# Half of each unit's attention moved beside the older unit's gate/value matmuls, with ScalarE's copies left to the scheduler

## The chip, the cores and the metric

One core of one Trainium2 chip runs the whole program. The metric is the device time of one execution in microseconds (us); the median of the runs is what the prediction is about.

## What is computed

A gated linear recurrence over 4 batches, 8 heads and 768 time steps of width 48 feeds a GEGLU block with a gated residual over 3072 tokens of width 384:

```
mag = sqrt(a_re² + a_im²);  a = (a_re + i·a_im) · min(mag, 0.999) / (mag + 1e-6)
S_t = a_t ∘ S_{t-1} + k_t v_tᵀ          (complex state, 48×48 per head)
x_t = q_t · Re(S_t)                      (heads side by side: 384 numbers per token)
out = x + sigmoid(x w_res) · ((gelu(x w_gate) · (x w_val)) w_out)      (d_ff 1536)
```

## The kernel before

The recurrence is done as attention within chunks of 128 tokens, with a carried state between chunks. A **chunk** is 128 tokens of all 8 heads; a **group** g is two chunks; a **unit** u is two groups, that is four chunks or 512 tokens. There are 6 units, 12 groups (3 to a batch) and 24 chunks. The program walks u from -2 to 6 and traces two stages for each value, `phase_x(u)` (called the **X stage** here) and `phase_y(u)` (the **Y stage**).

The X stage of u holds work for four units at once. For u+2 it makes the logarithm of the magnitude (`lm`) and the tangent of the phase (`th`), lines 148 to 171: six table functions of ScalarE for each group (Ln, Exp, Square, Ln, later Arctan), with VectorE's products between. For u+1 it makes the running sums along time by matmul (`csl`, `cst`, lines 174 to 210), their exponentials `E` and `Ei`, the reduced phases `fg`, and at the end the Sin functions `CS` (lines 212 to 217). For each group of u+1 that is not the first of its batch it sends three rows through DRAM on GpSimd's DMA queue (`md`, then `m3`, printed as `m_` with a number, lines 219 to 237) to get the factor `M` by which the carried state is brought to the new group's origin. For u it runs the attention of all four chunks (lines 260 to 338), and for u-1 the output matmuls `op` (lines 382 to 392).

Attention of one chunk is two half-chunks of four heads. Each transposes Q and K on TensorE into one PSUM tile `tp`, which ScalarE and VectorE copy in turn into `qk` (lines 278 and 279); then TensorE makes the scores `at`, VectorE masks them into `atm` (line 286), and TensorE makes `y`. `tp`, `at` and `y` have one PSUM buffer each. ScalarE casts `y` to `x`, TensorE transposes it (`tpx`), and ScalarE or VectorE copies it into `xT` (lines 351 and 353), the input of the dense block. `dk` is the state's new part, `G` and `Gb` the carried state.

The Y stage of u runs the gate/value matmuls of u: 12 steps of three matmuls into `gp` and three into `vp` (lines 355 to 370, 128 by 512 each), a Gelu on ScalarE and a product on VectorE for each, and four steps `rp` for the residual gate. `gp`, `vp`, `rp`, `op`, `csl` and `cst` share four PSUM buffers. The Y stage also makes the products for u+1 on VectorE (`qE`, `kE`, `Q`, `K`, lines 239 to 257) and issues the loads.

ScalarE needs three table sets in turn: logarithm and exponential, Arctan and Sin, Gelu and Tanh; each switch is an ACT_TABLE_LOAD (line 397). The order of work is set as follows. `weave` (line 17) sorts steps by a position in the stage; a scheduler then orders every engine's instructions when the program is built, except ScalarE's, which `tc.manual_schedule` (line 452) keeps in the traced order, its copies included. SP issues the loads of q, k, a_re (`ar`) and a_im (`ai`) and the stores, GpSimd those of v, the weights and `md`. At the start SP's queue holds `ar` and `ai` of groups 0 to 3 and then q and k.

Of the kernel before, what the change touches and what calls it, by code (L numbers as in the profile page):

```python
# [28 lines left out]
def kernel(  # L29
# [118 lines left out]
    def p1_steps(g):  # L148
        def s0():
            T["lm", g] = pA.tile([128, W], FP, tag="lm", name="lm")  # L150
            nc.scalar.activation(out=T["lm", g], in_=flat(T["ar", g]), func=AF.Ln)  # L151

        def s1():
            T["th", g] = pA.tile([128, W], FP, tag="th", name="th")
            nc.scalar.activation(out=T["th", g], in_=T["lm", g], func=AF.Exp, scale=-1.0)  # L155
            nc.vector.tensor_tensor(out=T["th", g], in0=T["th", g], in1=flat(T["ai", g]), op=OP.mult)  # L156

        def s2():
            T["s", g] = pS.tile([128, W], FP, tag="s", name="s")
            nc.scalar.activation(out=T["s", g], in_=T["th", g], func=AF.Square)  # L160

        def s3():
            nc.scalar.activation(out=T["s", g], in_=T["s", g], func=AF.Ln, bias=1.0)
            lm = T["lm", g]
            nc.vector.scalar_tensor_tensor(out=lm, in0=T["s", g], scalar=0.5, in1=lm, op0=OP.mult, op1=OP.add)
            nc.vector.tensor_scalar(out=lm, in0=lm, scalar1=LNMAX, scalar2=None, op0=OP.min)  # L166

        return [s0, s1, s2, s3]

    def p1_arctan(g):  # L170
        nc.scalar.activation(out=T["th", g], in_=T["th", g], func=AF.Arctan)


    def cs_l(g, c):
        if c == 0:
            T["E", g] = pE.tile([128, W], FP, tag="E", name="E")
            T["Ei", g] = pE.tile([128, W], FP, tag="Ei", name="Ei")
        sl = slice(c * DM, (c + 1) * DM)
        cs = psM.tile([128, DM], FP, tag="mm", padded_shape=[128, 512], name="csl")
        nc.tensor.matmul(out=cs, lhsT=lmat[c], rhs=T["lm", g][:, sl], start=True, stop=True)  # L180

        def ex():
            nc.scalar.activation(out=T["E", g][:, sl], in_=cs, func=AF.Exp)
            nc.scalar.activation(out=T["Ei", g][:, sl], in_=cs, func=AF.Exp, scale=-1.0)  # L184
        return ex
# [26 lines left out]
    def p2_sin(g):  # L212
        T["CS", g] = pQ.tile([128, C * H, 2, D], BF, tag="CS", name="CS")

        nc.scalar.activation(out=T["CS", g][:, :, 0], in_=T["fg", g][:, :, 0], func=AF.Sin, scale=2.0 * math.pi,
                             bias=hpi)
        nc.scalar.activation(out=T["CS", g][:, :, 1], in_=T["fg", g][:, :, 1], func=AF.Sin, scale=2.0 * math.pi)

    def decay(g):
# [40 lines left out]
    def attention(g, c):  # L260
        s = g % NS
        first = s == 0 and c == 0
        Q = T["Q", g].rearrange("p x u d -> p x (u d)")
        K = T["K", g].rearrange("p x u d -> p x (u d)")
        V = T["v", g]
        st = {}

        def grp(hg):
            def a():
                tp = psT.tile([128, 1024], BF, tag="tp", name="tp")  # L270
                for j in range(4):
# [16 lines left out]
            return a  # L288

        def dk():  # L290
            if s == NS - 1 and c == C - 1:
# [4 lines left out]
            for h in range(H):  # L296
                nc.tensor.matmul(out=d[0:DD, h * D:(h + 1) * D], lhsT=K[:, c * H + h], rhs=V[:, c, h],
                                 start=(c == 0 and h == 0), stop=(h == H - 1), skip_group_check=True)

        def yy():  # L300
            y = psY.tile([128, DM], FP, tag="y", padded_shape=[128, 512], name="y")
            for h in range(H):
                ys = y[:, h * D:(h + 1) * D]
                hg, j = divmod(h, 4)
                nc.tensor.matmul(out=ys, lhsT=st["atm", hg][:, j], rhs=V[:, c, h], start=True, stop=first)  # L305
                if not first:
# [4 lines left out]
            T["x", g * C + c] = x  # L311

        def state():
            if s == NS - 1 and c == C - 1:
                return
            d = T["dk", g][0:DD].rearrange("p (h d) -> p h d", h=H)
            Gb = stt.tile([128, H, D], BF, tag="Gb", name="Gb")
            if c == 0:
                if s == 0:
# [35 lines left out]
    def gv_step(u, ffi):  # L355
# [12 lines left out]
        nc.scalar.activation(out=h2[:, ffi, :], in_=gp, func=AF.Gelu)  # L368
        nc.vector.scalar_tensor_tensor(out=h2[:, ffi, :], in0=h2[:, ffi, :], scalar=0.5, in1=vp,
                                       op0=OP.mult, op1=OP.mult)  # L370

    def rp_step(u, jj):
# [7 lines left out]
        nc.scalar.activation(out=T["sg", u][:, jj], in_=rp, func=AF.Tanh, scale=0.5)  # L380

# [13 lines left out]
    def table(nm):  # L395
        def f():
            nc.scalar.preload_act_table_set(nm)  # L397
        return f
# [7 lines left out]
    def zip_steps(lists):  # L406
        return [st for tup in zip(*lists) for st in tup]

    def phase_x(u):

# [5 lines left out]
        def ex():  # L416
            pend.pop(0)()
        front = []
        for g in gs(u + 1):
            for c in range(C):  # L420
                front.append(call(csl, g, c))
        p1 = zip_steps([p1_steps(g) for g in gs(u + 2)])
# [4 lines left out]
        trig = [table("trig_and_small")] + [call(p1_arctan, g) for g in gs(u + 2)] + [call(p2_sin, g) for g in gs(u + 1)]  # L427
        att = [st for g in gs(u) for c in range(C) for st in attention(g, c)]
        ops = [call(op_step, u - 1, jj) for jj in range(4)] if 0 <= u - 1 < NU else []
        xts = []  # L430
        if gs(u):
            att2 = []
            for i in range(4):
                att2 += att[4 * i:4 * i + 4] + [call(xt_step, u, i)]
            att = att2
        if p1 or exs:
            table("natural_log_exp_and_others")()
        weave((0.0, 0.12, front), (0.05, 0.55, p1), (0.15, 0.5, exs), (0.5, 0.5, dec), (0.25, 0.7, cst),
              (0.69, 0.69, dec2), (0.7, 0.95, trig), (0.0, 1.0, att), (0.1, 1.1, ops))

    def phase_y(u):
# [6 lines left out]
        pr = [st for g in gs(u + 1) for st in products(g)]  # L448
        lds = [call(load_a, g) for g in gs(u + 4)] + [call(load_q, g) for g in gs(u + 3)]
        weave((0.0, 1.0, gv), (0.0, 0.8, pr), (0.0, 0.6, lds))  # L450

    with tc.manual_schedule(engines={mybir.EngineType.Activation}):
        for g in gs(0) + gs(1):
            load_a(g)
        for g in gs(0):
            load_q(g)
        for u in range(-2, NU + 1):
            phase_x(u)
            if u == -2:
                for g in gs(1):  # L460
                    load_q(g)
                load_w()
            phase_y(u)

# [29 lines left out]
```

## Time and profile before

| what | value |
|---|---|
| time, median of 3 runs | 428.3 us (427.64 to 428.71) |
| time of the profiled execution | 427.52 us |
| its span, first to last instruction | 425.8 us |
| busy: TensorE, VectorE, ScalarE | 72%, 60%, 49% of the span |
| start to the first X stage with attention (u = 0) | 71 us |
| X stage of u = 0, which has no `op` beside it | 44.5 us |
| from the first gate/value matmul of one unit to that of the next | 57.8, 59.3, 58.6, 54.8, 48.4 us |
| last Y stage and last four `op` steps | 18.6 and 12.8 us |

A stage is read from the trace by the first gate/value matmul of its unit and the last residual matmul. Busy time of TensorE counts pipelined matmuls by their full latency, so start-to-start distances tell more there. The granted clock is TensorE's mean clock as a share of 2.4 GHz; the two levels are 1.2 and 2.4 GHz.

### The profile page before, as it was taken

The page shows a single profiled execution, that of the slowest core. Times are in us where ns is not written, and L with a number is a line of the kernel's source. Part 1 is how long each engine was busy: PE and PEld are TensorE (multiplying, and loading weights), DVE is VectorE, ACT ScalarE, POOL GpSimd, SP SyncE. Part 2 cuts the span into 40 slices and gives each one's busy share as a digit, 9 for nine tenths or more (in the row PEclk, how much of TensorE's full clock was granted, in tenths as well). Part 3 has the DMA queues.
Part 4 walks back from the last instruction along what each step waited for, and adds up shares of the span by engine and source line. Part 5 has one row for each costly group of instructions (what it writes and reads, how often), then busy time and mean ns, then how long its engine had stood idle before and what let it go on. Part 6 is the DMA issues. An engine that isn't in the chain of part 4 may idle for free.

```text
span 425.8 us, 5538 instructions
## 1 busy us (share of the span) xinstructions
PE 307.9 (72%) x2080; PEld 176.0 (41%) x2080; DVE 254.7 (60%) x452; ACT 209.7 (49%) x342; POOL 58.5 (14%) x88
## 2 busy tenths in 40 slices
PE   0040361664699895898966997958989879975996
PEld 0020121443445463445544455634456534654353
DVE  1310385578853598744898435997536974672344
ACT  1530618454746657457447366574553555424450
POOL 9330150022100240100311002100004000000000
PEclk9985585575599898799985898976998969995799
DMA  9999999999860791802364500211001100010002
GB/s 140 158 201 174 164 155 182 185 156 166 140 62 2 130 147 42 94 0 39 79 57 95 70 0 1 76 49 26 0 3 21 38 20 0 20 57 0 1 2 74
DMA packets 145146, 32.22 MB, mean 76 GB/s; under 512 B 139360, under 2 KB 144352, under 8 KB 145120
## 3 DMA queue, kind: packets, MB, share of 16 engines
q1 hardware_dynamic: 111616, 25.17, 34.8%
q0 software_dynamic: 33504, 6.70, 18.6%
q8 instruction: 16, 0.26, 0.3%
q14 instruction: 10, 0.08, 0.1%
HBM read 33.69 MB, written 4.76 MB: 90 GB/s over the span
## 4 chain that ended last, share of the span: by engine, by line
PE 54%; DVE 18%; issue 8%; DMA 8%; ACT 8%; POOL 3%; DVEq 0%; POOLq 0%; ACTq 0%
PE gp L362 13%; PE vp L366 12%; PE op L386 8%; DMA wr<-in_moe_w_res_dram 4%; DVE atm L286 3%; PE cst L200 3%; PE at L283 3%; PE rp L378 3%; PE csl L180 2%; DMA v<-in_v_dram 2%; PE tp L273 2%; PE tp L276 2%; PE cst L202 2%; DVE qk L279 2%; POOL v L132 2%
## 5 line engine op out<-in xcount | busy, mean ns | idle before, releaser
L362 PE MATMUL gp<-xT,wg 128*128 128x512 bf16 x216 | 65.2, 415 | 2.7 <-DVE xT L353 2.7
L366 PE MATMUL vp<-xT,wv 128*128 128x512 bf16 x216 | 63.8, 407 | 0.0
L278 ACT COPY qk<-tp 96x512 bf16<-96x512 bf16 x48 | 27.9, 581 | 47.0 <-PE tp L276 46.9
L156 DVE TENSOR_TENSOR th<-th,ai 128x768 f32<-128x768 f32 x12 | 11.5, 958 | 47.2 <-ACT th L155 40.3
L286 DVE TENSOR_TENSOR atm<-at,mask_81 128x512 bf16<-128x512 f32 x48 | 33.0, 687 | 10.3 <-PE at L283 10.2
L283 PE MATMUL at<-qk 96*128 96x128 bf16 x192 | 22.1, 248 | 22.4 <-DVE qk L279 22.2
L362 PEld LDWEIGHTS <-wg 128*128 128x128 bf16 x216 | 22.7, 105 | 31.4 <-issue 11.3
L366 PEld LDWEIGHTS <-wv 128*128 128x128 bf16 x216 | 22.5, 104 | 30.1 <-issue 8.1
L310 ACT CAST x<-y 128x384 bf16<-128x384 f32 x24 | 11.5, 479 | 47.5 <-PE y L307 39.9
L273 PE MATMUL tp<-ident,Q 128*96 128x128 bf16 x192 | 22.3, 249 | 17.1 <-DVE Q L254 9.8
L279 DVE COPY qk<-tp 96x512 bf16<-96x512 bf16 x48 | 20.0, 417 | 23.8 <-ACT qk L278 23.7
L132 POOL DMA_DIRECT2D v<-in_v_dram x28 | 25.1, 905 | 51.9 <-PE y L307 46.6
L200 PE MATMUL cst<-th,lt0b 128*128 128x384 f32 x24 | 13.1, 631 | 22.1 <-ACT Ei L184 21.7
L273 PEld LDWEIGHTS <-Q 128*96 128x96 bf16 x192 | 19.2, 148 | 23.4 <-issue 11.0
L397 ACT ACT_TABLE_LOAD x22 | 28.2, 1283 | 1.1 <-PEq L478 0.7
L283 PEld LDWEIGHTS <-qk 96*128 96x128 bf16 x192 | 13.4, 108 | 34.8 <-DVE qk L279 33.1
L180 PE MATMUL csl<-lm,lt0a 128*128 128x384 f32 x24 | 11.3, 556 | 22.7 <-DVE lm L166 22.7
L151 ACT ACTIVATE lm<-ar 128x768 f32<-128x768 f32 x12 | 10.1, 842 | 31.8 <-DMA ar<-in_a_re_dram 31.8
L305 PE MATMUL y<-v,atm 128*128 128x48 bf16 x192 | 17.8, 196 | 10.6 <-DVE atm L286 10.6
L276 PE MATMUL tp<-ident,K 128*96 128x128 bf16 x192 | 22.5, 251 | 0.2 <-DVE K L254 0.2
L223 POOL DMA_DIRECT2D md<-Ei x8 | 4.0, 506 | 123.2 <-ACT Ei L184 123.2
L305 PEld LDWEIGHTS <-atm 128*128 128x128 bf16 x192 | 12.9, 103 | 19.1 <-DVE atm L286 17.5
(124 smaller groups left out, 641.5 us busy)
## 6 DMA issues: line engine op xcount, KB each, us to landing
q<-in_q_dram SPq DMA_DIRECT2D x28, 192.0 KB, 4.6
k<-in_k_dram SPq DMA_DIRECT2D x28, 192.0 KB, 4.7
ar<-in_a_re_dram SPq DMA_DIRECT2D x24, 192.0 KB, 4.5
ai<-in_a_im_dram SPq DMA_DIRECT2D x24, 192.0 KB, 4.9
out_dram<-ot SPq DMA_DIRECT2D x24, 192.0 KB, 1.9
v<-in_v_dram POOLq DMA_DIRECT2D x28, 96.0 KB, 6.1
wg<-in_moe_w_gate_dram POOLq DMA_DIRECT2D x3, 384.0 KB, 14.7
wv<-in_moe_w_val_dram POOLq DMA_DIRECT2D x3, 384.0 KB, 15.5
```

Of the source, the lines that this page charges most:

```text
L132: nc.gpsimd.dma_start(out=t[:, c], in_=rows(v, g, c))
L273: nc.tensor.transpose(out=tp[0:DD, j * 128:j * 128 + 128], in_=Q[:, x], identity=ident)
L276: nc.tensor.transpose(out=tp[0:DD, 512 + j * 128:640 + j * 128], in_=K[:, x], identity=ident)
L278: nc.scalar.copy(out=qk[0:DD, 0:512], in_=tp[0:DD, 0:512])
L279: nc.vector.tensor_copy(out=qk[0:DD, 512:1024], in_=tp[0:DD, 512:1024])
L283: nc.tensor.matmul(out=at[:, j], lhsT=qk[0:DD, 512 + j * 128:640 + j * 128], rhs=qk[0:DD, j * 128:j * 128 + 128], start=True, stop=True)
L286: nc.vector.tensor_tensor(out=atm, in0=at, in1=mask4, op=OP.mult)
L305: nc.tensor.matmul(out=ys, lhsT=st["atm", hg][:, j], rhs=V[:, c, h], start=True, stop=first)
L362: nc.tensor.matmul(out=gp, lhsT=wg[:, fi, ffi * 128:(ffi + 1) * 128], rhs=xT[:, fi, :], start=(fi == 0), stop=(fi == KD - 1))
L366: nc.tensor.matmul(out=vp, lhsT=wv[:, fi, ffi * 128:(ffi + 1) * 128], rhs=xT[:, fi, :], start=(fi == 0), stop=(fi == KD - 1))
L386: nc.tensor.matmul(out=ps, lhsT=h2[:, ffi, jj * 128:(jj + 1) * 128], rhs=wo[:, ffi, :], start=(ffi == 0), stop=(ffi == KF - 1))
L397: nc.scalar.preload_act_table_set(nm)
```

## The change

Attention is cut by groups. The first group of unit u+1 (two chunks, 256 tokens) is traced in the Y stage of u, from 0.3 to 0.95 of it; the second group of u stays in the X stage of u, from 0 to 0.8. The products for u+1 are pressed into the first 0.4 of the Y stage. All attention steps are given high priority in the scheduler. `tc.manual_schedule` goes: ScalarE's instructions are scheduled like the others', only that a chain of added dependences without semaphores (`tab`) keeps table loads and all table functions in traced order; plain copies (`qk`, `x`, `xT`) are free. The carried state is multiplied by `M` at the entry of the next group (`enter`) and not at the end of the last one. Pools: `x` 8 to 10 buffers, `xT` 1 to 2, `m3` and `M` 2 to 3. SP's first loads now go a group at a time: `ar`, `ai`, q, k of group 0, then of group 1, then the rest. Every table function of ScalarE is traced through the helper `act` (so the changed kernel's rows for them show its line, L120).

```diff
+    def tab(ins):
+        if "tab" in T:
+            tc.add_manual_dep(ins.ins, T["tab"].ins.name, order, reason="table order")
+        T["tab"] = ins
+
+    def act(**kw):
+        tab(nc.scalar.activation(**kw))
...
+        def hi(f):
+            def w():
+                with tc.high_priority():
+                    f()
+            return w
+        return [hi(f) for f in (enter, grp(0), dk, grp(1), yy)]
...
+    def att_steps(u, half):
+        steps = []
+        for g in gs(u)[half:half + 1]:
+            for c in range(C):
+                steps += attention(g, c)
+                steps.append(call(xt_step, u, half * C + c))
+        return steps
...
-        weave((0.0, 0.12, front), (0.05, 0.55, p1), (0.15, 0.5, exs), (0.5, 0.5, dec), (0.25, 0.7, cst),
-              (0.69, 0.69, dec2), (0.7, 0.95, trig), (0.0, 1.0, att), (0.1, 1.1, ops))
+        weave((0.0, 0.12, front), (0.05, 0.55, p1), (0.12, 0.45, exs), (0.46, 0.46, dec), (0.25, 0.65, cst),
+              (0.69, 0.69, dec2), (0.7, 0.95, table_trig), (0.0, 0.8, att_steps(u, 1)), (0.1, 1.0, ops))
...
-        weave((0.0, 1.0, gv), (0.0, 0.8, pr), (0.0, 0.6, lds))
-    with tc.manual_schedule(engines={mybir.EngineType.Activation}):
+        weave((0.0, 1.0, gv), (0.0, 0.4, pr), (0.3, 0.95, att_steps(u + 1, 0)))
+    for g in gs(0):
+        load_a(g)
+        load_q(g)
+    for g in gs(1):
+        load_a(g)
+    for g in gs(1):
+        load_q(g)
...
```

**ScalarE in the X stage of u = 1.** Before, from the last two `E` to the first of the Sin functions; the copies `qk`, `xT` and the cast `x` belong to attention.

```order
L183 ACTIVATE E<-csl 128x384
L184 ACTIVATE Ei<-csl 128x384
L163 ACTIVATE s<-s 128x768 x2
L278 COPY qk<-tp 96x512 x2
L310 CAST x<-y 128x384
L233 ACTIVATE m_1210<-m_1210 96x8
L233 ACTIVATE m_1217<-m_1217 96x8
L397 ACT_TABLE_LOAD
L351 COPY xT<-tpx 128x3x128
L171 ACTIVATE th<-th 128x768
L278 COPY qk<-tp 96x512
L171 ACTIVATE th<-th 128x768
```

The changed kernel in the same place, from the third pair of `E` and `Ei`:

```order
L120 ACTIVATE Ei<-csl 128x384
L120 ACTIVATE s<-th 128x768
L372 COPY xT<-tpx 128x3x128
L120 ACTIVATE s<-th 128x768
L120 ACTIVATE E<-csl 128x384
L295 COPY qk<-tp 96x512
L120 ACTIVATE Ei<-csl 128x384
L120 ACTIVATE s<-s 128x768 x2
L295 COPY qk<-tp 96x512
L120 ACTIVATE m_1258<-m_1258 96x8
L120 ACTIVATE m_1265<-m_1265 96x8
L418 ACT_TABLE_LOAD
```

The stage has four copies `qk` in place of eight, each with table functions between it and the next; between the third `Ei` and the first `m_` row six table functions, two copies `qk` and one `xT` stand.

**TensorE and VectorE in the Y stage of u = 1.** Before, VectorE's row for the Gelu products of this unit comes once, then one `Gb`, then 11 times without anything between. In the changed kernel attention of u = 2 stands between; TensorE first (rows that repeat are left out), then VectorE:

```order
L293 MATMUL tp<-ident,K 96x128
...
L300 LDWEIGHTS qk
L300 MATMUL at<-qk 128x128
...
L387 LDWEIGHTS wv
L387 MATMUL vp<-xT,wv 128x512
...
L338 LDWEIGHTS atm
L338 MATMUL y<-v,atm 128x48
L340 LDWEIGHTS qk
L340 MATMUL y<-Gb,qk 128x48
```

```order
L390 SCALAR_TENSOR_TENSOR h_1413<-h_1413,vp 128x512 x2
L351 TENSOR_TENSOR Gb<-dk,G 96x384
L296 COPY qk<-tp 96x512
L390 SCALAR_TENSOR_TENSOR h_1413<-h_1413,vp 128x512
L316 TENSOR_TENSOR G<-dk,G 96x384
L303 TENSOR_TENSOR atm<-at,mask_81 128x512
L317 TENSOR_TENSOR G<-G,M 96x384
L296 COPY qk<-tp 96x512
L390 SCALAR_TENSOR_TENSOR h_1413<-h_1413,vp 128x512
L303 TENSOR_TENSOR atm<-at,mask_81 128x512
L253 TENSOR_TENSOR qE<-q,E 128x768
```

Gate/value matmuls stand between a step of attention and the step that needs its result, on TensorE; on VectorE copies, masks and products stand between the Gelu products.

**SP's loads at the start.** Before:

```order
L121 DMA ar_151<-in_a_re_dram 128x8x48 x2
L121 DMA ai_154<-in_a_im_dram 128x8x48 x2
L121 DMA ar_157<-in_a_re_dram 128x8x48 x2
L121 DMA ai_160<-in_a_im_dram 128x8x48 x2
L121 DMA ar_163<-in_a_re_dram 128x8x48 x2
L121 DMA ai_166<-in_a_im_dram 128x8x48 x2
L121 DMA ar_169<-in_a_re_dram 128x8x48 x2
L121 DMA ai_172<-in_a_im_dram 128x8x48 x2
L128 DMA q_175<-in_q_dram 128x8x48 x2
```

The changed kernel (`ar_188` is group 3's):

```order
L132 DMA ar_152<-in_a_re_dram 128x8x48 x2
L132 DMA ai_155<-in_a_im_dram 128x8x48 x2
L139 DMA q_158<-in_q_dram 128x8x48 x2
L139 DMA k_161<-in_k_dram 128x8x48 x2
L132 DMA ar_167<-in_a_re_dram 128x8x48 x2
L132 DMA ai_170<-in_a_im_dram 128x8x48 x2
L139 DMA q_173<-in_q_dram 128x8x48 x2
L139 DMA k_176<-in_k_dram 128x8x48 x2
L132 DMA ar_182<-in_a_re_dram 128x8x48 x2
L132 DMA ai_185<-in_a_im_dram 128x8x48 x2
L132 DMA ar_188<-in_a_re_dram 128x8x48 x2
```

The loads of q and k of groups 0 and 1, eight transfers, stand ahead of `ar` of group 2 where they stood behind `ai` of group 3.

## Rows read from the trace of the kernel before

**Rows 1.** Windows by stage: us, busy of PE, PEld, DVE, ACT, POOL (instructions), PEclk, DMA, GB/s
```profile
71.00:115.50 44.50, 26.39 (x216) 19.58 (x217) 34.04 (x61) 25.36 (x42) 6.19 (x9) 0.58 1.15 163
...
133.50:173.30 39.80, 31.40 (x268) 19.89 (x266) 30.97 (x60) 25.55 (x44) 8.55 (x12) 0.87 0.57 86
173.30:191.30 18.00, 18.00 (x79) 7.99 (x79) 9.69 (x14) 8.29 (x15) 0.50 (x1) 0.92 0.47 54
...
251.80:291.20 39.40, 30.58 (x270) 20.43 (x269) 31.26 (x60) 25.35 (x42) 3.72 (x6) 0.84 0.17 41
...
310.00:346.00 36.00, 30.01 (x268) 19.43 (x267) 26.21 (x53) 18.48 (x34) 4.93 (x7) 0.92 0.10 24
...
364.80:394.40 29.60, 21.87 (x242) 15.02 (x241) 16.13 (x31) 10.72 (x18) 0.00 (x0) 0.83 0.08 28
```

**Rows 2.** Waits of the whole span: who waited for whom: us in total, times, longest
```profile
ACT qk L278 <- PE tp L276: 46.9, 28, 3.9
...
ACT x L310 <- PE y L307: 39.9, 20, 3.4
...
PE at L283 <- DVE qk L279: 22.2, 19, 3.3
...
PE y L305 <- DVE atm L286: 10.6, 16, 1.1
```

**Rows 3.** Groups by line: busy us, mean ns of one, idle before
```profile
L286 DVE TENSOR_TENSOR atm<-at,mask_81 128x512 bf16<-128x512 f32 x48 | 33.0, 687 | 10.3 <-PE at L283 10.2
...
L278 ACT COPY qk<-tp 96x512 bf16<-96x512 bf16 x48 | 27.9, 581 | 47.0 <-PE tp L276 46.9
...
L279 DVE COPY qk<-tp 96x512 bf16<-96x512 bf16 x48 | 20.0, 417 | 23.8 <-ACT qk L278 23.7
...
L310 ACT CAST x<-y 128x384 bf16<-128x384 f32 x24 | 11.5, 479 | 47.5 <-PE y L307 39.9
```

**Rows 4.** Timeline, ScalarE and GpSimd, stage X of u = 2: start, us, instruction
```profile
206.91 0.50 ACT L184 ACTIVATE Ei<-csl 128x384 f32<-128x384 f32 x1
...
210.30 0.87 POOL L227 DMA_DIRECT2D m_1858<-md  x1 [2.11 <-DVE qE L242]
```

**Rows 5.** View of the tile m_1858, its last line
```profile
DMA to landing us min/median/max: 4.4/4.4/4.4
```

**Rows 6.** Timeline of TensorE, stages X and Y of u = 2
```profile
203.92 0.39 PE L273 MATMUL tp<-ident,Q 128*96 128x128 bf16 x4
204.14 0.39 PE L276 MATMUL tp<-ident,K 128*96 128x128 bf16 x4
...
207.19 0.20 PE L305 MATMUL y<-v,atm 128*128 128x48 bf16 x1
207.22 0.18 PE L307 MATMUL y<-Gb,qk 96*128 96x48 bf16 x1
...
235.06 1.48 PE L362 MATMUL gp<-xT,wg 128*128 128x512 bf16 x3
...
242.22 0.81 PE L366 MATMUL vp<-xT,wv 128*128 128x512 bf16 x3
242.87 0.81 PE L362 MATMUL gp<-xT,wg 128*128 128x512 bf16 x3
```

**Rows 7.** Windows of 2 us in the stage X of u = 2, columns as in rows 1
```profile
206.00:208.00 2.00, 2.00 (x23) 1.21 (x22) 2.00 (x6) 2.00 (x5) 0.65 (x2) 1.00 0.28 99
...
222.00:224.00 2.00, 0.61 (x7) 0.50 (x6) 1.85 (x4) 1.99 (x3) 0.00 (x0) 0.50 0.30 108
```

**Rows 8.** Timeline of the start, SP's queue and ScalarE
```profile
44.42 4.62 SPq L128 DMA_DIRECT2D q<-in_q_dram  x2
46.65 0.84 ACT L151 ACTIVATE lm<-ar 128x768 f32<-128x768 f32 x1 [11.67 <-DMA ar<-in_a_re_dram]
...
55.15 2.77 SPq L128 DMA_DIRECT2D q<-in_q_dram  x2
...
65.57 0.21 ACT L233 ACTIVATE m_330<-m_330 96x8 f32<-96x8 f32 x1 [10.64 <-DMA m_330<-md]
```

More of the change, by code (lines that the diff above doesn't have):

```diff
@@ L109 @@
     T = {}
+    order = mybir.DependencyInfo(mybir.DependencyClass.NoSync, mybir.DependencyReason.DATA)
+    def tab(ins):
[4 more added lines that the diff above has]
+        tab(nc.scalar.activation(**kw))
     def rows(a, g, c):
@@ L170, in p1_arctan @@
     def p1_arctan(g):
-        nc.scalar.activation(out=T["th", g], in_=T["th", g], func=AF.Arctan)
+        act(out=T["th", g], in_=T["th", g], func=AF.Arctan)
     def cs_l(g, c):
@@ L182, in ex @@
         def ex():
-            nc.scalar.activation(out=T["E", g][:, sl], in_=cs, func=AF.Exp)
-            nc.scalar.activation(out=T["Ei", g][:, sl], in_=cs, func=AF.Exp, scale=-1.0)
+            act(out=T["E", g][:, sl], in_=cs, func=AF.Exp)
+            act(out=T["Ei", g][:, sl], in_=cs, func=AF.Exp, scale=-1.0)
         return ex
@@ L213, in p2_sin @@
         T["CS", g] = pQ.tile([128, C * H, 2, D], BF, tag="CS", name="CS")
-        nc.scalar.activation(out=T["CS", g][:, :, 0], in_=T["fg", g][:, :, 0], func=AF.Sin, scale=2.0 * math.pi,
+        act(out=T["CS", g][:, :, 0], in_=T["fg", g][:, :, 0], func=AF.Sin, scale=2.0 * math.pi,
                              bias=hpi)
-        nc.scalar.activation(out=T["CS", g][:, :, 1], in_=T["fg", g][:, :, 1], func=AF.Sin, scale=2.0 * math.pi)
+        act(out=T["CS", g][:, :, 1], in_=T["fg", g][:, :, 1], func=AF.Sin, scale=2.0 * math.pi)
     def decay(g):
@@ L288, in grp, with enter @@
             return a
+        def enter():
+            if s == 0 or c > 0:
+                return
+            d = T["dk", g - 1][0:DD].rearrange("p (h d) -> p h d", h=H)
+            Mb = T["M", g][0:DD].rearrange("p (h u) -> p h u", u=1).to_broadcast([DD, H, D])
+            G = stt.tile([128, H, D], FP, tag="G", name="G")
+            if s == 1:
+                nc.vector.tensor_tensor(out=G[0:DD], in0=d, in1=Mb, op=OP.mult)
+            else:
+                nc.vector.tensor_tensor(out=G[0:DD], in0=d, in1=T["G"][0:DD], op=OP.add)
+                nc.vector.tensor_tensor(out=G[0:DD], in0=G[0:DD], in1=Mb, op=OP.mult)
+            Gb = stt.tile([128, H, D], BF, tag="Gb", name="Gb")
+            nc.vector.tensor_copy(out=Gb[0:DD], in_=G[0:DD])
+            T["G"] = G
+            T["Gbf"] = Gb
         def dk():
@@ L296, in dk @@
             for h in range(H):
-                nc.tensor.matmul(out=d[0:DD, h * D:(h + 1) * D], lhsT=K[:, c * H + h], rhs=V[:, c, h],
+                nc.tensor.matmul(out=d[0:DD, h * D:(h + 1) * D], lhsT=K(c * H + h), rhs=V(h),
                                  start=(c == 0 and h == 0), stop=(h == H - 1), skip_group_check=True)
@@ L304, in yy @@
                 hg, j = divmod(h, 4)
-                nc.tensor.matmul(out=ys, lhsT=st["atm", hg][:, j], rhs=V[:, c, h], start=True, stop=first)
+                nc.tensor.matmul(out=ys, lhsT=st["atm", hg][:, j], rhs=V(h), start=True, stop=first)
                 if not first:
@@ L311, in yy @@
             T["x", g * C + c] = x
[L313 to L317, printed above, removed]
             if c == 0:
+                d = T["dk", g][0:DD].rearrange("p (h d) -> p h d", h=H)
+                Gb = stt.tile([128, H, D], BF, tag="Gb", name="Gb")
                 if s == 0:
@@ L367, in gv_step @@
                              start=(fi == 0), stop=(fi == KD - 1))
[L368 removed]
+        act(out=h2[:, ffi, :], in_=gp, func=AF.Gelu)
         nc.vector.scalar_tensor_tensor(out=h2[:, ffi, :], in0=h2[:, ffi, :], scalar=0.5, in1=vp,
@@ L379, in rp_step @@
                              start=(fi == 0), stop=(fi == KD - 1))
-        nc.scalar.activation(out=T["sg", u][:, jj], in_=rp, func=AF.Tanh, scale=0.5)
+        act(out=T["sg", u][:, jj], in_=rp, func=AF.Tanh, scale=0.5)
     def op_step(u, jj):
@@ L417, in ex @@
             pend.pop(0)()
[L418 to L421, printed above, removed]
+        front = [call(csl, g, c) for g in gs(u + 1) for c in range(C)]
         p1 = zip_steps([p1_steps(g) for g in gs(u + 2)])
@@ L427, in phase_x @@
         trig = [table("trig_and_small")] + [call(p1_arctan, g) for g in gs(u + 2)] + [call(p2_sin, g) for g in gs(u + 1)]
-        att = [st for g in gs(u) for c in range(C) for st in attention(g, c)]
         ops = [call(op_step, u - 1, jj) for jj in range(4)] if 0 <= u - 1 < NU else []
[L430 to L435, printed above, removed]
         if p1 or exs:
             table("natural_log_exp_and_others")()
-        weave((0.0, 0.12, front), (0.05, 0.55, p1), (0.15, 0.5, exs), (0.5, 0.5, dec), (0.25, 0.7, cst),
-              (0.69, 0.69, dec2), (0.7, 0.95, trig), (0.0, 1.0, att), (0.1, 1.1, ops))
+            table_trig = trig
+        else:
+            table_trig = []
+        weave((0.0, 0.12, front), (0.05, 0.55, p1), (0.12, 0.45, exs), (0.46, 0.46, dec), (0.25, 0.65, cst),
+              (0.69, 0.69, dec2), (0.7, 0.95, table_trig), (0.0, 0.8, att_steps(u, 1)), (0.1, 1.0, ops))
     def phase_y(u):
@@ L448, in phase_y @@
         pr = [st for g in gs(u + 1) for st in products(g)]
-        lds = [call(load_a, g) for g in gs(u + 4)] + [call(load_q, g) for g in gs(u + 3)]
-        weave((0.0, 1.0, gv), (0.0, 0.8, pr), (0.0, 0.6, lds))
-    with tc.manual_schedule(engines={mybir.EngineType.Activation}):
-        for g in gs(0) + gs(1):
-            load_a(g)
[L455 to L463, printed above, removed]
+        weave((0.0, 1.0, gv), (0.0, 0.4, pr), (0.3, 0.95, att_steps(u + 1, 0)))
[6 more added lines that the diff above has]
+        load_q(g)
+    for u in range(-2, NU + 1):
+        phase_x(u)
+        if u == -2:
+            load_w()
+        phase_y(u)
+        for g in gs(u + 4):
+            load_a(g)
+        if u >= -1:
+            for g in gs(u + 3):
+                load_q(g)
 _INS = ['q', 'k', 'v', 'a_re', 'a_im', 'moe_w_gate', 'moe_w_val', 'moe_w_out', 'moe_w_res']
```

50 lines of the change are left out of this document (20 added, 30 removed).

## The prediction

> **What bounds the kernel now.** I read four views in this order. The windows by stage come first [rows 1]: in an X stage no engine is full. Take those of u = 1 and u = 3 (that of u = 2, between them, is alike): in 39.4 to 39.8 us TensorE is busy for some 31, VectorE for some 31, ScalarE for 25.5. In the Y stage of u = 1 TensorE is busy all 18.0 us, VectorE 9.7, ScalarE 8.3. So the Y stage is TensorE's, with room on the two others, and the X stage belongs to something that is not busy time.
>
> The list of waits says to what [rows 2]. ScalarE, which ran in traced order, waited 46.9 us for the transposes `tp` before its copies `qk` and 39.9 us for `y` before its casts `x`. That is 86.8 us over 24 chunks, 3.6 us for each, 14.5 us for the four of an X stage. Busy 25.5 and waits 14.5 make 40.0, which is the stage's length. The X stage is ScalarE's queue: a copy that waits for TensorE holds up every table function behind it, and a table function holds up the copy on which TensorE's next step waits. From the first gate/value matmul of u = 0 to that of u = 3 (115.5 to 291.2 us [rows 1]) there are three periods of one Y and one X stage: 175.7 us, 58.6 each.
>
> **The change, part by part.** The sum is made against the profiled execution, 427.5 us (span 425.8 and 1.7 around it), 0.8 below the median of the runs.
>
> *X stage, u = 1 to 3.* Two of four chunks leave it. ScalarE loses four `qk` of 0.58, two `x` of 0.48 [rows 3] and one `xT` that I count as an `x`: 3.8 us, so 21.7 are left. The waits for the two chunks that stay would be 7.2 us at the old price; by the order of the changed kernel each `qk` now has table functions before the next, and only table functions must keep their order. The bounds are 0 and 7.2; I take half, 3.6, since nothing in the trace says how well the scheduler's idea of a duration fits. A wait shows that the long stage hid: the factor that comes back through DRAM. In u = 2 the `Ei` ended at 207.4; the first `m3` transfer was issued at 210.3, the second 0.87 later, and landed 4.4 after that, at 215.6 [rows 4, 5]: 8.2 us. In the changed order there stand between this `Ei` and the `m_` row four table functions of 0.84 (the `lm` row has their size [rows 8]), `E` and `Ei` of 0.5 [rows 4], two `qk` and one `xT`: 6.0 us. ScalarE then waits 2.2 ahead of the Sin table. Sum: 21.7 + 3.6 + 2.2 = 27.5 us. VectorE loses 4 × (0.69 + 0.42) = 4.4 [rows 3] of its 31 and part of the products, so it stays just under that; TensorE is below both. Bounds: 23.9 (no attention wait) and 31.1 (7.2 of it).
>
> *Y stage, u = 0 to 4.* TensorE's 18.0 stay. As `gp` and `vp` share four buffers, two steps (four tiles, 0.65 each from start to start [rows 6]) can run while ScalarE is still at the Sin functions: 2.6 off, since `xT` of u is now ready earlier than the tables are. Two chunks come in. At full clock four transposes start 0.22 after the four before them, and one `y` matmul 0.03 after another [rows 6]; a chunk has 27 matmuls of 128 columns and 24 of 48: 1.5 + 0.7 = 2.2 us, two chunks 4.4. TensorE runs in order and so waits where a result is late: before, 22.2 us for `qk` and 10.6 for `atm` [rows 2] over 48 half-chunks, 0.7 each; four make 2.7. Sum: 18.0 − 2.6 + 4.4 + 2.7 = 22.5. VectorE's load there is 9.7 + 4.4 and part of the products, and stays below. Lower bound 19.8 (no waits). Upper bound: two chunks at the price that one has when it stands nearly alone, 29.6 / 4 = 7.4 in the X stage of u = 5 [rows 1]: 18.0 − 2.6 + 14.8 = 30.2. I take 22.5 because the order puts gate/value matmuls between each attention step and its user, as nothing did in u = 5.
>
> A rule speaks against this stage. The row first: with attention, `op` and `cst` mixed, TensorE was granted full clock in 206 to 208 us, and half in 222 to 224, where it was busy only 0.61 of 2 us [rows 7]. The Trainium skill (TensorE: Matmul & The Clock Gate, section A second HAM failure mode: psum-queue depth-cycling) says that frequent short idles between groups of 512-column matmuls make the clock swing between its levels. By it the Y stage would lose its full clock; by the row it keeps it as long as TensorE stays busy.
>
> A period is then 27.5 + 22.5 = 50.0 instead of 58.6: three times 8.6, **−25.8 us**.
>
> *Y of u = 3 and X of u = 4.* X was 36.0 with ScalarE busy 18.5 [rows 1]; 14.7 are left. There is no work for later units, so less covers the DRAM trip, and two factors are wanted: I put 7 for that wait and 1.8 for attention, 23.5. With Y 46.0 against 54.8: **−8.8**.
>
> *Y of u = 4 and X of u = 5.* X was 29.6 us for four chunks with little beside them; two cost 14.8, with 1.2 for the handover 16.0. With Y 38.5 against 48.4: **−9.9**. Two of the table loads go here as well, inside this term.
>
> *X of u = 0.* Nothing runs beside it, so all four chunks stay in line. The two halves of its ScalarE order are freer: at most the 14.5 us of waits, at least nothing. VectorE is busy 34.0 of 44.5 [rows 1], which caps the gain at 10. I take **−5**.
>
> *Start.* q and k of groups 0 and 1 move ahead of `ar` of group 2. SP took from 44.42 to 55.15 to issue those eight [rows 8]: 10.7 us. The `lm` that begins the first long chain started at 46.65 after a wait of 11.7 for its `ar` [rows 8]; it would come up to 10.7 later. But that chain then waited 10.6 us for `m_330` [rows 8], a trip on another queue, part of which takes up the delay. Bounds +2 and +12; I take **+7**.
>
> *Costs nothing:* `enter` does on VectorE what the end of the last group did; the added buffers take room only; the last Y stage and the last `op` steps (31.4 us) have the same work.
>
> Sum: −25.8 − 8.8 − 9.9 − 5 + 7 = −42.5, hence 385.0 for the profiled execution and **386** as median.
>
> **The rivals.**
>
> *Attention is serialised in the Y stage (slower).* TensorE executes in order. If the copies wait behind Gelus on ScalarE and behind products on VectorE, every half-chunk holds up the gate/value matmuls and a chunk costs its 7.4. Y is then 30.2. If the X stage, as ScalarE's queue, stands at its upper bound of 31.1, the period is 61.3: three times +2.7, u = 4 about +2, u = 5 (30.2 + 16 against 48.4) −2, start +7, nothing gained at u = 0, in all +15: 443 us. A period grows from 7.9 us a chunk with X at 27.5, from 6.1 with X at 31.1. For it: both engines get 12 Gelus and products that stand between. Against: both are under half busy in Y.
>
> *The clock falls in the Y stage (slower).* By the rule above as a mechanism here: three 512-column matmuls take 1.48 at half clock and 0.81 at full [rows 6], 0.67 more; 24 triples make 16 us a stage, five stages 80, less the 42: 466 us. The page is the one named. Against it stand the rows of a mixed stretch at full clock [rows 7].
>
> *Half the gain.* X stays near 31 (the waits move from `tp` and `y` to the DRAM factor and to VectorE, which at 27 of busy time is close to the bound), and Y is 25: period 56, −2.6 three times, −4, −6, −3, and the start costs +7: about 412.
>
> *More than forecast.* X at its lower bound of 24 and Y at 20.5, 44.5 together: −14 three times, −12, −12, −8 and +3: 357; half way to it is 371.
>
> *It does not do what it says.* That attention would be put behind the gate/value matmuls is excluded by the order: its steps stand among them.
>
> **How the numbers follow.** A measurement of this kernel can tell some 0.3% from no change, 1.3 us. The forecast as above, 374 to 400: 0.64. Half the gain, 400 to 424: 0.14. More, below 374: 0.10. Serialised: 0.06. Clock: 0.03. No change to be told: 0.02; a later start larger than a small gain: 0.01. Faster is 0.64 + 0.14 + 0.10 = 0.88, same 0.02, slower 0.10. The range 371 to 412 leaves out about half of the larger gain, the end of the smaller and all that is slower, some 0.2.
>
> **What would show it.** Period 50 from gate/value matmul to gate/value matmul; waits of ScalarE for `tp` and `y` under half of their 86.8; a new wait of ScalarE for an `m_` transfer in each X stage; TensorE's granted clock near full in Y, and Y 22 to 23 us long; the first gate/value matmul at 114 to 121 us instead of 115.5; the last 31 us as before. The prediction is wrong if X of u = 1 to 3 is above 31, if Y is above 26, or if the first gate/value matmul comes after 125.

## The result, and the profile after

| | before | after |
|---|---|---|
| time, median of 4 runs each | 428.5 us (427.64 to 429.22) | 384.2 us (381.31 to 386.25) |
| ratio after/before, 95% interval | | 0.896 (0.889 to 0.903) |
| profiled execution; its span | 427.52; 425.8 us | 382.5; 380.7 us |
| mean granted TensorE clock | 0.823 | 0.924 |
| first Gelu of u = 0 | 117.0 us | 118.0 us |
| period, from first Gelu to first Gelu, u = 0 to 5 | 57.7, 59.3, 58.7, 54.7, 48.5 | 52.1, 47.9, 49.8, 46.6, 36.3 |
| from the first Gelu of u = 5 to the end | 29.9 | 30.0 |

One of the four executions of start_order, below, fell in the chip's slower state (381.3 us), so its time there is the median of the other three.

The windows by stage of the changed kernel (columns as in [rows 1]): Y of u = 0, X and Y of u = 1, X and Y of u = 2, X of u = 3.

```profile
118.00:139.50 21.50, 21.34 (x166) 11.81 (x168) 12.50 (x21) 11.97 (x22) 1.76 (x2) 1.00 0.07 4
139.50:170.00 30.50, 22.24 (x152) 13.30 (x152) 20.07 (x41) 21.15 (x35) 7.20 (x10) 0.89 0.81 111
170.00:193.20 23.20, 22.87 (x191) 13.02 (x193) 20.66 (x36) 12.35 (x23) 1.80 (x2) 1.00 0.26 47
193.20:217.90 24.70, 20.91 (x156) 12.69 (x156) 19.00 (x38) 21.03 (x35) 6.56 (x8) 0.93 0.62 86
217.90:241.00 23.10, 22.98 (x198) 13.16 (x199) 21.18 (x36) 12.71 (x24) 0.00 (x0) 1.00 0.32 61
241.00:267.70 26.70, 20.90 (x154) 12.25 (x154) 21.93 (x44) 20.71 (x33) 3.71 (x6) 0.94 0.24 54
```

Y is still TensorE's: busy 22.98 of 23.10 us, at a granted clock of 1.00, with attention inside. X of u = 1 to 3 fell from 39 to 40 us [rows 1] to 30.5, 24.7 and 26.7, with ScalarE busy some 21 in each.

ScalarE's waits over the span of the changed kernel (columns as in [rows 2]):

```profile
ACT qk L295 <- PE tp L293: 18.7, 20, 2.1
ACT x L343 <- PE y L340: 11.5, 8, 2.9
...
ACT CS L120 <- DVE fg L220: 10.3, 5, 5.0
...
ACT m_313 L120 <- DMA m_313<-md: 7.7, 1, 7.7
...
ACT m_1265 L120 <- DMA m_1265<-md: 4.5, 1, 4.5
ACT m_1258 L120 <- DMA m_1258<-md: 4.2, 1, 4.2
ACT m_1914 L120 <- DMA m_1914<-md: 3.4, 1, 3.4
```

The waits for `tp` and `y` went from 86.8 us [rows 2] to 30.2. New in the X stages are waits for the factor out of DRAM and for `fg` of VectorE (the 7.7 for `m_313` lie at the start, where the kernel before waited 10.6 [rows 8]). ScalarE in X of u = 1 shows where the first kind lies (start, us, instruction, idle before it): two in a row, since both groups of unit 2, for which this stage works, need a factor, and behind them the switch of tables, and so the Sin functions and the Gelus.

```profile
152.09 0.59 ACT L295 COPY qk<-tp 96x512 bf16<-96x512 bf16 x1
156.92 0.21 ACT L120 ACTIVATE m_1258<-m_1258 96x8 f32<-96x8 f32 x1 [4.24 <-DMA m_1258<-md]
161.67 0.21 ACT L120 ACTIVATE m_1265<-m_1265 96x8 f32<-96x8 f32 x1 [4.54 <-DMA m_1265<-md]
161.90 1.28 ACT L418 ACT_TABLE_LOAD   x1
```

### The profile page after: what moved, and what is told of

Its sections match the earlier page's. It is cut to its first block, busy times and chain, and to the rows that moved or that the text cites. A ratio compares the mean times of both kernels' runs of the same rounds, so it can differ in the third digit from the quotient of the medians.

```text
span 380.7 us, 5497 instructions
## 1 busy us (share of the span) xinstructions
PE 278.4 (73%) x2059; PEld 162.7 (43%) x2080; DVE 247.6 (65%) x452; ACT 205.6 (54%) x340; POOL 56.0 (15%) x84
## 4 chain that ended last, share of the span: by engine, by line
PE 35%; DVE 7%; ACT 6%; issue 5%; DMA 5%; POOL 1%; POOLq 0%; ACTq 0%; DVEq 0%
PE gp L383 10%; PE vp L387 10%; PE op L407 5%; PE rp L399 3%; ACT L418 2%; DMA md<-Ei 1%; PE tp L290 1%; PE at L300 1%; PE tp L293 1%; ACT th L120 1%; PE dk L330 1%; PE y L338 1%; DMA m_3114<-md 1%; DVE ot L410 1%; DMA m_2530<-md 1%
## 5 line engine op out<-in xcount | busy, mean ns | idle before, releaser
L383 PE MATMUL gp<-xT,wg 128*128 128x512 bf16 x203 | 60.7, 388 | 5.0 <-DVE xT L374 3.8
L387 PE MATMUL vp<-xT,wv 128*128 128x512 bf16 x208 | 60.9, 387 | 0.2
L191 PE MATMUL csl<-lm,lt0a 128*128 128x384 f32 x24 | 11.4, 562 | 49.7 <-DVE lm L177 49.7
L295 ACT COPY qk<-tp 96x512 bf16<-96x512 bf16 x48 | 27.9, 582 | 20.7 <-PE tp L293 18.7
L143 POOL DMA_DIRECT2D v<-in_v_dram x24 | 22.0, 932 | 71.2 <-PE y L340 71.2
L383 PEld LDWEIGHTS <-wg 128*128 128x128 bf16 x216 | 20.4, 99 | 23.2 <-issue 6.0
L120 ACT ACTIVATE lm<-ar 128x768 f32<-128x768 f32 x12 | 9.7, 838 | 38.0 <-DMA ar<-in_a_re_dram 38.0
L296 DVE COPY qk<-tp 96x512 bf16<-96x512 bf16 x48 | 19.9, 415 | 14.8 <-ACT qk L295 14.5
L387 PEld LDWEIGHTS <-wv 128*128 128x128 bf16 x216 | 20.5, 100 | 20.7 <-issue 2.9
L290 PE MATMUL tp<-ident,Q 128*96 128x128 bf16 x192 | 20.3, 233 | 11.6 <-DVE qk L296 6.6
L191 PEld LDWEIGHTS csl<-lm,lt0a 128*128 128x128 f32 x24 | 4.7, 212 | 52.8 <-DVE lm L177 47.5
L410 DVE SCALAR_TENSOR_TENSOR ot<-sg,op 128x384 f32<-128x384 f32 x24 | 13.1, 546 | 11.7 <-PE op L407 11.7
L300 PE MATMUL at<-qk 96*128 96x128 bf16 x192 | 20.0, 230 | 0.7 <-DVE qk L296 0.6
L368 PE MATMUL tpx<-ident,x 128*128 128x128 bf16 x72 | 9.1, 235 | 12.0 <-ACT x L343 12.0
```

The lines of the kernel that those rows point to most:

```text
L143: nc.gpsimd.dma_start(out=t[:, c], in_=rows(v, g, c))
L295: nc.scalar.copy(out=qk[0:DD, 0:512], in_=tp[0:DD, 0:512])
L296: nc.vector.tensor_copy(out=qk[0:DD, 512:1024], in_=tp[0:DD, 512:1024])
L300: nc.tensor.matmul(out=at[:, j], lhsT=qk[0:DD, 512 + j * 128:640 + j * 128], rhs=qk[0:DD, j * 128:j * 128 + 128], start=True, stop=True)
L383: nc.tensor.matmul(out=gp, lhsT=wg[:, fi, ffi * 128:(ffi + 1) * 128], rhs=xT[:, fi, :], start=(fi == 0), stop=(fi == KD - 1))
```

## The experiments

Ratios are to the kernel before, timed beside each, with 95% intervals. The first two take the change apart.

**lift_only: ScalarE's order freed, attention not moved.**

```diff
-(0.0, 0.8, att_steps(u, 1))
+(0.0, 1.0, att_steps(u, 0) + att_steps(u, 1))
-weave((0.0, 1.0, gv), (0.0, 0.4, pr), (0.3, 0.95, att_steps(u + 1, 0)))
+weave((0.0, 1.0, gv), (0.0, 0.8, pr))
```

> All four chunks stay in the X stage (spread over the whole of it); ScalarE is freed from traced order as in the changed kernel, pools and loads are the changed kernel's. Theory A (ScalarE's fixed order was the cost): X of u = 1 to 3 is 25.5 busy plus half of the 14.5 us of waits, 33 us, Y 16 to 18 us, a period 49 to 51; X of u = 5 stays near 29 because four chunks in line remain; 395 us in all. Theory B (attention has to stand beside the gate/value matmuls; alone in X its chain of copies keeps its length): X stays at 36 to 38, a period 54 to 56, 410 to 415 us.

Measured: 431.9 us, ratio 1.008 (1.006 to 1.011); first Gelu at 119.3; periods 67.3, 59.4, 56.7, 51.9, 46.1; start, pools and priorities are the changed kernel's. ScalarE's waits, and two windows of it (the end of X of u = 2; then up to the next table load):

```profile
ACT qk L295 <- PE tp L293: 42.0, 31, 3.0
...
ACT x L343 <- PE y L340: 34.8, 14, 4.0
...
ACT m L120 <- DMA m<-md: 25.4, 7, 8.2
```

```profile
235.60:245.90 10.30, 7.26 (x69) 5.76 (x69) 8.55 (x15) 2.91 (x4) 1.78 (x2) 0.50 0.69 95
245.90:265.80 19.90, 19.80 (x106) 10.04 (x107) 9.87 (x15) 10.10 (x19) 0.00 (x0) 0.94 0.05 4
```

With the order free, the two waits are 76.8 us, against 86.8. At 235.60 ScalarE has done all its table functions and loads the Gelu table, but the chunks are not done: for 10.3 us more they are finished at half clock, with ScalarE busy 2.91. VectorE is busy 8.55 of these 10.3 us. Neither time was met (395, or 410 to 415). Theory A falls; B was right that X keeps its length, though it came out longer still. The freed order adds a cost of its own, the waits for the factor (9.6, 2.7 and 1.4 us in X of u = 1 to 3); but less these waits the periods would still be 55 to 58, not A's 49 to 51.

**move_only: attention moved, ScalarE in traced order.** The loop over u and the loads stand in `tc.manual_schedule` as before:

```diff
+with tc.manual_schedule(engines={mybir.EngineType.Activation}):
     for g in gs(0):
...
```

> Attention half a unit ahead as in the changed kernel, but ScalarE keeps traced order throughout. Theory A: X of u = 1 to 3 is 21.7 busy + 7.2 of attention waits + 2.2 for the DRAM factor, 31 us; in Y copies and Gelus wait for each other in a fixed order, 25 to 30 us; a period 56 to 61, 415 to 440 us. Theory B: the place alone brings it, the period is 50 to 52 and the time 385 to 395 us.

Measured: 374.2 us, ratio 0.876 (0.870 to 0.882); periods 48.6, 47.4, 47.9, 44.1, 35.7. That is theory B, and 11 us under its range: the gain comes without the freed order. With ScalarE free in both, the changed kernel and lift_only differ in the place of attention and in where the steps stand that make room for it: 384.2 against 431.9 us. With attention moved in both, the changed kernel and move_only differ in ScalarE's order: freeing it costs 9 to 10 us (0.020 of the time before by the ratios, whose intervals are apart). Traced order with the new pools, loads and priorities but with all four chunks in X was not run, so what these bring in that order is known for the dropped load alone (before_one_load, below). Where the freed order costs time, the same view hints at for move_only:

```profile
ACT x L343 <- PE y L340: 33.6, 20, 3.4
ACT qk L295 <- PE tp L293: 17.0, 22, 2.2
ACT m L120 <- DMA m<-md: 15.7, 4, 8.3
```

By these two rows it waits 20 us more for `y` and `tp` than the changed kernel, and it is faster. X of u = 1, from table load to Gelu table load, is 25.9 us, with 2.6 of wait for the factor; in the changed kernel 28.7, with 8.8.

**move_three and move_one: three chunks, or one, beside the gate/value matmuls.** In move_only,

```diff
-for g in gs(u)[half:half + 1]:
-    for c in range(C):
+for jj in (range(AHEAD) if half == 0 else range(AHEAD, 4)):
+    for g in gs(u)[jj // C:jj // C + 1]:
```

with `AHEAD` 3 or 1.

> move_only with three of the four chunks beside the older unit's gate/value matmuls and one left in the X stage. Theory C (the X stage lasts as long as its chunks take one after the other, about 10 us each beside the other work; lift_only showed that ScalarE's order is not it): X of u = 1 to 3 falls from 29.5 by up to 6, to ScalarE's and VectorE's busy time, while Y grows by a chunk's TensorE time and waits, 3.5; periods 45 to 47 instead of 48, X of u = 5 down by 6, 360 to 370 us. Theory A, mended (ScalarE's work moves with the chunks and sets both stages): a period stays at 48 to 50, 374 to 382.

> move_only with one chunk of four moved beside the gate/value matmuls and three left in the X stage. The periods of u = 1 to 3 were 58.6 with four chunks in X, 48.0 with two, 53.0 with one. If the X stage is set by its chunks one after the other as long as there are three, the period is about 53 and the time 395 to 403. If the other work of X (some 28 us) sets it with three already, each chunk moved only lengthens Y, and the period is 45 to 47: 362 to 371.

Measured: 399.7 us, ratio 0.934 (0.931 to 0.937), and 391.6, 0.917 (0.914 to 0.921). X and Y of u = 2, each from table load to table load, first of the kernel before, then of move_one, move_only and move_three:

```profile
193.00:231.60 38.60, 29.21 (x261) 19.06 (x259) 30.27 (x57) 23.33 (x40) 5.84 (x9) 0.81 0.41 68
231.60:253.30 21.70, 21.25 (x91) 9.58 (x92) 11.35 (x17) 10.37 (x18) 1.50 (x2) 0.86 0.39 46
```

```profile
189.10:218.10 29.00, 24.45 (x197) 14.54 (x196) 24.34 (x47) 21.27 (x35) 7.25 (x10) 0.91 0.50 70
218.10:239.80 21.70, 21.20 (x146) 11.20 (x145) 15.58 (x26) 12.21 (x22) 0.00 (x0) 0.96 0.41 73
```

```profile
189.80:215.40 25.60, 22.30 (x163) 12.90 (x162) 21.58 (x42) 19.86 (x34) 6.31 (x9) 0.95 0.70 92
215.40:237.70 22.30, 22.07 (x182) 12.45 (x184) 18.06 (x31) 13.24 (x25) 0.00 (x0) 0.98 0.27 57
```

```profile
207.90:229.00 21.10, 15.91 (x109) 9.47 (x109) 16.63 (x34) 18.01 (x29) 5.50 (x8) 0.97 0.48 76
229.00:259.40 30.40, 28.31 (x240) 16.28 (x242) 23.80 (x41) 15.21 (x28) 0.00 (x0) 0.97 0.29 60
```

| chunks in X, beside Y | X of u = 1, 2, 3 | Y of u = 1, 2, 3 |
|---|---|---|
| 4, 0 (before) | 37.2, 38.6, 36.9 us | 20.7, 21.7, 21.4 us |
| 3, 1 (move_one) | 28.3, 29.0, 28.7 | 22.6, 21.7, 21.4 |
| 2, 2 (move_only) | 25.9, 25.6, 25.6 | 21.8, 22.3, 23.1 |
| 1, 3 (move_three) | 26.0, 21.1, 22.0 | 30.8, 30.4, 31.0 |

X: with four and with three chunks it comes to 9.2 to 9.7 us a chunk (38.6 / 4, 29.0 / 3), and the fourth costs 8.2 to 9.6. The third costs only 2.4 to 3.4, so by then X is in part set by other work; by which was not tested (with one chunk ScalarE is busy 18.01 of 21.1). Some of the step from four to three can be the clock, granted 0.81 and then 0.91, or the other edits of the change, which the kernel before lacks. lift_only has those edits and four chunks: from its table load at 205.77 to its first Gelu are 40.1 us, in move_one, with three and in traced order, 30.3.

Y: in u = 2 the first two chunks cost 0.6 together (1.1 as the mean of the three), while the granted clock rises from 0.86 to 0.98; the third costs 8.1, with TensorE already full.

No expectation of these two runs was met. The period of move_one is 50.6 (the mean of 49.7, 51.6 and 50.4), between the two. For move_three theory C had Y wrong (8.1 more, not 3.5), and X, too, by the measure in which it was 29.5, from the last Gelu of a unit to the first of the next: 29.8, 28.9 and 29.5 became 32.7, 27.9 and 28.9. What left X between its table loads came back behind the last Gelu.

**factor_first and move_factor: the Exp ahead of the trip.** In the changed kernel and in move_only (`elp` is a pool of two buffers):

```diff
+el = elp.tile([1, DM], FP, tag="el", name="el")
+act(out=el, in_=T["lm", g][0:1, 0:DM], func=AF.Exp)
-nc.gpsimd.dma_start(out=md[2:3, :], in_=T["lm", g][0:1, 0:DM])
+nc.gpsimd.dma_start(out=md[2:3, :], in_=el)
-act(out=m3[0:DD, 2], in_=m3[0:DD, 2], func=AF.Exp)
-(0.69, 0.69, dec2)
+(0.97, 0.97, dec2)
```

> The changed kernel, with the Exp of the lm row taken before the trip through DRAM instead of after it, so that no table function waits for an m_ transfer (VectorE still does, at the end of the stage). If these waits (4.2, 4.5 and 3.4 us in X of u = 1 and 2, 7.7 at the start, 2.7 in u = 4) end the X stages, the time falls by some 10 us or more, to 365 to 375, and X of u = 1 and 2 are each 3 to 8 us shorter. If something else (the fg rows of VectorE, the loads) ends them just after, the time stays at 381 to 386.

> move_only (half a unit ahead, ScalarE in traced order, 374.2 us) with the Exp of the lm row taken before the trip through DRAM, as in factor_first. If the order of ScalarE and the wait for the factor are separate costs, both gains add: 374 less the m_ waits left in move_only (15.7 us, 8.3 of them at the start) or half of that, 360 to 368. If they are one cost (in traced order the copies fill the wait), 372 to 376.

Measured: 377.1 us, ratio 0.881 (0.877 to 0.885), and 378.1, 0.884 (0.880 to 0.887). In the changed kernel the edit takes off 7 us, half of it in the period that held the two waits (52.1 to 48.6 us); that is less than the 10 expected, while the waits of `CS` for `fg` grew from 10.3 to 23.2. In traced order it takes off nothing (periods 49.3, 47.4, 47.8, and 3.9 us more in all): X of u = 1 to 3 keeps its length from last to first Gelu, 29.8, 28.9 and 29.5 in both, as ScalarE waits for `y` instead. So the wait lengthens X only in the freed order. It is not all that this order costs: from the first Gelu of u = 0 to that of u = 5 the freed order took 232.7 us and takes 228.6 with the edit, the traced one 223.6 and 225.1; that the two times now agree (377.1 and 378.1) comes from a later start in traced order (first Gelu at 122.6 instead of 117.0).

**start_order, before_one_load, move_start: the loads of the start.** `ar` and `ai` of groups 0 to 3 first, in the changed kernel and in move_only; and, in the kernel before, without the second load of q, k and v of unit 1, which the change had dropped too:

```diff
-for g in gs(0):
+for g in gs(0) + gs(1):
     load_a(g)
+for g in gs(0) + gs(1):
     load_q(g)
...
-[call(load_q, g) for g in gs(u + 3)]
+[call(load_q, g) for g in gs(u + 3) if u >= -1]
```

> The changed kernel (384.2 us) with a_re and a_im of units 0 and 1 loaded ahead of all q, k and v, as the kernel before did. If the order on the load queue delays the start (the prediction's +7; its profile shows +3.9 at the table for the first Sin), the second lm starts at some 12 us instead of 38 and the first gate/value matmul 2 to 6 us earlier, 378 to 382. If the start is bound by the bytes that have to come in, or by the trip of the factor, it stays at 384 to 386.

> The kernel before, with the second load of q, k and v of unit 1 left out (2 MB of 32). If the loads of the start are hidden, 427 to 429 us as before. If the fewer loads were part of the gain of the changed kernel, the start is earlier by up to 6 us (first gate/value matmul at 110 to 115 instead of 115.5) and the time 422 to 426.

> move_only with a_re and a_im of units 0 and 1 loaded first, as in start_order. The two edits lie in different places (the start, the periods of u = 1 to 5), so both gains should stand: 374.2 - 7.5 = 366 to 368 us, first Gelu at 110 to 113 instead of 120.7, periods of 47 to 49. If in traced order the start hangs on something else (its trip of the factor, the q and k that now come later), 371 to 375.

Measured: start_order 376.0 us, ratio 0.879 (0.875 to 0.883), a little better than expected, first Gelu at 109.5 instead of 118.0; before_one_load 423.3, 0.989 (0.985 to 0.993), first Gelu at 112.4 instead of 117.0; move_start 368.4, 0.864 (0.860 to 0.868), first Gelu at 113.2 instead of 120.7 and periods as in move_only. The second `lm` of the changed kernel, then of start_order:

```profile
38.40 0.84 ACT L120 ACTIVATE lm<-ar 128x768 f32<-128x768 f32 x1 [32.67 <-DMA ar<-in_a_re_dram]
```

```profile
12.75 0.84 ACT L120 ACTIVATE lm<-ar 128x768 f32<-128x768 f32 x1 [6.98 <-DMA ar<-in_a_re_dram]
```

**late_w and move_start_late: the weights later.** late_w traces the weight loads later; move_start_late, made from move_start, traces them a stage later and ties each to the last transfer of a trip (`md` to `m3`, unit 0's here), so that it is issued after it.

```diff
+ins = nc.gpsimd.dma_start(**kw)
+tc.add_manual_dep(ins.ins, T["trip"].ins.name, order, reason="weights after the trip")
```

> The changed kernel with the weights (gate, value and residual) issued after the decay trips of unit 0 and the output weights one stage later, instead of all in the first 10 us. If the first 70 us are bound by bytes (the profile shows the 16 queues busy all that time, at 150 to 200 GB/s, and the weights are 7.7 MB of it), the first gate/value matmul comes 10 to 25 us earlier: 360 to 374. If the chain of the start sets it, no change, 384; if the weights then come too late for the gate/value matmuls, later: 385 to 400.

> move_start with every weight load held back until the DRAM trip of unit 0 has been issued (in late_w only the output weights had really moved, from 20 to 46 us; the others were still issued at 9 to 19 us). If the start is bound by bytes, unit 0's lm, which waited until 44 us for its a_re in start_order, come by 15 to 30 us, and the first Gelu at 85 to 105: 345 to 362 us. If the chain of the start sets it, as move_start, 366 to 368; if the weights come too late for the first gate/value matmul, up to 380.

Measured: late_w 383.9 us, ratio 0.898 (0.892 to 0.904), which doesn't answer the question, since the scheduler put the gate and value loads back to 9 us and only the output weights came later. move_start_late 358.7, ratio 0.840 (0.836 to 0.844), the fastest of all: its first weight load is issued at 39.91 us and its first Gelu comes at 103.1, 10 us earlier than in move_start. The second `lm` of unit 1 (the expectation calls it unit 0's), which waits for its `ar`, starts at 29.09 instead of 44.26 us. The bytes of the start were part of what bound it.

**before_tp2: two buffers for `tp`.** In the kernel before,

```diff
-name="psM", bufs=4
+name="psM", bufs=3
-name="psT", bufs=1
+name="psT", bufs=2
```

> The kernel before, with two PSUM buffers for the transposes tp and three instead of four for the other matmuls. Nothing of ScalarE's order changes. If the X stage of before is the chain of chunks through single buffers, X of u = 5 (nothing beside, 29.6 us) falls by 2 to 5 us and X of u = 1 to 3 by 1 to 4, while Y may grow by 0 to 3 for the lost buffer: 412 to 428. If ScalarE's traced order sets it, X stays within 0.5 us: 427 to 440.

Measured: 420.0 us, ratio 0.983 (0.979 to 0.987). From the last Gelu to the next stage's first, X of u = 5 falls from 31.1 to 25.6 us. There four chunks stand nearly alone, and the single `tp` buffer is part of the stage's length. X of u = 1 to 3 gives no answer: 41.2, 42.6 and 40.9 became 47.2, 39.6 and 41.9.

## Why the prediction was right

The time (386 forecast, 384.2 measured) and the sum of nearly every stage came out, but the mechanism given for the largest was wrong, and in its terms two errors cancel. So the hit is in part luck.

**The stages.** Three periods were to give −25.8 us; from the first Gelu of u = 0 to that of u = 3 they gave 175.7 − 149.7 = 26.0. X was put at 27.5 (measured 30.5, 24.7, 26.7, mean 27.3), Y at 22.5 (21.5 for u = 0, then 23.2, 23.1). u = 4: −8.8 forecast, −8.1 measured. u = 5: −9.9 and −12.2. Start and X of u = 0: +2 and +1.0. The last part: unchanged, as said. A slip on the side: under "Half the gain" the terms add up to −13.8, which makes some 414, not 412.

**The terms of X.** ScalarE's busy time was put at 21.7 and is 21.0 in the mean. For attention 3.6 us of waits were put in; in the three windows of X above they are 0, 0 and 0.4. For the factor 2.2 were put in; the waits for the factor and for `fg` are 8.8, 3.6 and 5.5. Together 5.8 were forecast and 6.1 came: the freed order did take the attention waits out of X, below the half that was assumed, and other waits took their place. X of u = 1 is the longest because it needs two factors, which the prediction counted only for u = 4. GpSimd issues the two trips one behind the other: the second one's transfers into `m_1265` start at 157.7 us and land by 161.6, 14 us after the end of the `Ei` that they need, where 8.2 were counted. In Y the 2.7 for TensorE's waits didn't come either (it is idle for 0.1 to 0.3 us), so that 22.5 is right as a sum only.

**The step that failed** is "The X stage is ScalarE's queue", and with it the halving of the attention waits "since only table functions must keep their order". lift_only frees that order, and the three periods are 67.3, 59.4 and 56.7 us where they were 57.7, 59.3 and 58.7; its stages end with chunks that ScalarE's table functions no longer hold up. That busy 25.5 and waits 14.5 add up to 40.0 shows only that ScalarE was either busy or waiting all the time, not that it set the pace. What the runs showed in its place: with four or three chunks X is as long as they take, 9.2 to 9.7 us each. The change takes two of the four away, and with that, in traced order (move_only), the period is 48.0. Why a chunk takes 9.7 us beside other work, and 7.4 nearly alone [rows 1], isn't settled. before_tp2 shows the single `tp` buffer as part of it only where the chunks stand alone. The half clock and VectorE's queue are rivals that no run tests: VectorE masks and copies for every chunk, is busy for 30.27 of the 38.6 us of X before, and 8.55 of the 10.3 in lift_only's tail.

**Freeing the order** is a cost, which the prediction booked as a gain. The wait for the factor was foreseen (2.2 us in each X; measured 8.8, 3.4 and none in u = 1 to 3), but it was put down to the shorter stage ("a wait shows that the long stage hid"), and factor_first against move_factor says that it costs only in the freed order. Why a scheduler's order runs into it is argued: it goes by durations foreseen when the program is built, and where a transfer or VectorE is later than foreseen, the engine stands with ready copies behind.

**The clock** was a rival, with the sign the wrong way round. TensorE was granted 1.00 in the Y stages of u = 0 to 2 that hold attention, and over the span 0.924 instead of 0.823; it fell to 0.50 where chunks ran nearly alone on TensorE (the tail of lift_only, TensorE busy 7.26 of 10.3 us). The rule of the Trainium skill (TensorE: Matmul & The Clock Gate, section A second HAM failure mode: psum-queue depth-cycling) that the prediction weighed was not put to the test: in Y the trace shows hardly any of the short idles that it speaks of (TensorE busy 22.98 of 23.10 us), and no swing followed. TensorE's busy time for one X and Y of u = 2 went from 50.5 us in the kernel before to 44.4 in move_only. The prediction had no term for that.

**The start** was two terms that nearly cancel. At the first table load of X of u = 0 the load order costs 6.8 us (75.67, in start_order 68.86), near the +7; but 3.1 come back by the load that was dropped (before 71.80, in before_one_load 68.73), which the prediction did not see, and the difference, 3.7, is about the 3.9 by which this load came later than before. From there to the first Gelu X of u = 0 gained 2.9 (45.2 to 42.3), not 5.

**The serialised rival** didn't come: Y is 21.5 to 23.2 us, not 30.2. With a third chunk in Y (move_three) Y is 30.4, but the agreement says nothing for the rival, since TensorE is busy 28.31 of them and not waiting.

## What to carry to other kernels

A sum of busy time and waits that equals a stage's length does not say that this engine sets the stage: free the engine alone and look, and count the waits that freeing it adds. When a chain of dependent steps sets one stage and TensorE another, move steps of the chain over, and measure the split from both sides; here two of four was the best. A duplicated load, or one put ahead of the load that the first chain waits for, is paid for at the start, here with 4.6 and 8.5 us at the first Gelu.

## What was not expected

Keeping ScalarE in the order as written was worth 9 to 10 us once attention was moved, though it then waits longer for `y` and `tp`. Loading the weights only when unit 0's trip was out gave another 10 us. Together with the old order of the first loads (move_start_late) that is 358.7 us: 0.840 of the kernel before, and faster than the changed kernel, too.
